# Row-tiling the w_phi folds of a one-core attention and feed-forward kernel

## The chip, the cores and the metric

One Trainium2 chip, one core. The metric is the device time of one execution in microseconds (us). All executions quoted here were in the same (fast) state, at a granted TensorE clock of 0.999 to 1.0 of full speed. The kernel before takes 288.41 us in the median of six runs (287.72 to 289.37).

PE is TensorE (matmuls), PEld its weight loads, DVE VectorE, ACT ScalarE, SP SyncE, which only issues DMAs here.

## The reference, cut to what matters

```python
# A: linear attention with a learned feature map, 32 heads of 20 features; B: gated feed-forward
pq = einsum("bhsd,hdf->bhsf", q, w_phi)      # the same for k
phi_q = concat([softmax(pq), softmax(-pq)])
...
out = g * A(x) + (1 - g) * B(x)              # x is 2048 x 640
```

The kernel never computes q. It folds w_phi into the projection weights once: wq2 = wq @ BD, where BD holds the 20 x 20 block of each head on its diagonal. This fold is small: five row blocks of 128 rows for k and five for q. After it come the projections, the attention state, the feed-forward products (gate, up, down), and the attention output, which joins the down product.

## The kernel before: the parts that the change and the argument touch

One fold multiplies a 128-row block of weights by BD. The 640 features are five groups of 128, and 128 is no multiple of 20, so a group touches seven or eight heads. Heads 0 to 15 go to one bank of the result memory (PSUM), heads 16 to 31 to another; the middle group is split. The function, simplified:

```python
def fold(self, kt, which, banks, ekey):
    for i in range(self.KD):                       # 5 feature groups of 128
        lo, hi = self.HLO[i], self.HHI[i]          # heads that the group touches
        for h in (0, 1):                           # two banks
            a, z = max(lo, 16 * h), min(hi, 16 * h + 15)
            if a > z: continue
            n = (z - a + 1) * DH                   # 140 columns, 80 for the split group
            matmul(bank(banks[h])[:, c0:c0 + n], wT[:, i, kt*P:(kt+1)*P], self.BD[:, i, k0:k0 + n], ...)
    # then one copy out of PSUM (an evacuation), by VectorE ("d") or ScalarE ("a")
```

The order around the folds (v_early and k_early are projections, 128-row matmuls):

```python
self.v_early(4, 6); self.v_early(5, 0)
f(0, "k", (2, 3), "d"); f(1, "k", (4, 5), "a")
self.v_early(6, 6)
f(2, "k", (2, 3), "d"); f(3, "k", (4, 5), "a"); f(4, "k", (0, 1), "d")
self.v_early(7, 6); self.k_early(0, 2)
f(0, "q", (4, 5), "d"); f(1, "q", (6, 7), "d")
self.k_early(1, 0)
f(2, "q", (4, 5), "d"); f(3, "q", (6, 7), "d")
self.k_early(2, 2)
f(4, "q", (4, 5), "d")
...                                              # k_early(3), then pq: the q projections
```

For each of 16 row tiles, `num(t)` computes the attention numerator on PE (64-row matmuls), normalises it on DVE, about 4 us, and issues a DMA that transposes the result into goT. The output matmuls of the tile read goT later. The list `at` says at which of the 148 steps of a stage of four tiles (185 in the last) a numerator is put; a step is two matmuls and takes 0.135 us.

```python
def num(self, t):
    ...                                          # 20 matmuls, 11 VectorE operations
    sc.dma("sp", lambda e: e.dma_start_transpose(self.goT[:, gs, :, :], self.Og[:, sl, :]), ...)

def first_nums(idx):                             # in the second gate and up stage
    if idx in (4, 8):
        self.num(idx // 4 - 1)                   # tiles 0 and 1
...
at = (1, 31, 61, 91)
for b in range(self.NB):
    downs(b, {at[k]: 4 * b + 2 + k for k in range(4 if b < 3 else 2)})
```

The softmax here doesn't subtract the row's maximum and nothing guards it: scores larger than these inputs give would overflow.

## Time and profile before

| quantity | value | where it stands |
|---|---|---|
| time | 288.41 us | median of 6 runs |
| PE busy | 281.2 of 286.9 us | the table of busy time |
| folds, first to last | 13.8 to 24.3 us | the line of the folds, L332 |
| down stage, first to last matmul start | 197.93 to 283.88 us: 85.95 us | single records |

Four lines from the page of the kernel before: the span, busy time with its share and the number of instructions, then the chain of work that ended last, as shares of the span by engine and by line (L352 are the projections and the gate and up products, L714 the down and output products, L658 the numerators, L332 the folds).

```profile
span 286.9 us, 7006 instructions
PE 281.2 (98%) x3017; PEld 185.5 (65%) x3032; DVE 174.7 (61%) x353; ACT 105.0 (37%) x199; POOL 5.3 (2%) x36
...
PE 93%; SPq 3%; DMA 2%; ACT 1%; issue 1%; ACTq 0%
PE ps L352 60%; PE ps L714 28%; PE ps L658 2%; DMA xT<-in_A_x_dram 2%; PE ps L450 2%; SPq L221 2%; PE ps L332 1%; SPq L234 1%; SPq L225 1%; ACT Ek L414 0%; ACT Eq L519 0%; SPq L217 0%; ACT outsb L727 0%; ACT gcol L417 0%; ACTq L42 0%
```

The kernel is bound by PE, and the folds hold 1% of the chain. Next, PE's timeline around the folds: start, duration, form, count; a bracket shows idle time and what ended it.

```profile
13.84 0.79 PE L332 MATMUL ps<-BD,wkT 128*128 128x140 bf16 x12
14.80 1.53 PE L352 MATMUL ps<-w,xT 128*128 128x512 bf16 x10 [0.18 <-DMA xT<-in_A_x_dram]
16.18 1.11 PE L332 MATMUL ps<-BD,wkT 128*128 128x140 bf16 x18
...
20.01 0.80 PE L332 MATMUL ps<-BD,wqT 128*128 128x140 bf16 x12
20.65 1.53 PE L352 MATMUL ps<-w,xT 128*128 128x384 bf16 x10
22.01 0.79 PE L332 MATMUL ps<-BD,wqT 128*128 128x140 bf16 x12
22.64 1.52 PE L352 MATMUL ps<-w,xT 128*128 128x384 bf16 x10
```

The pair of folds at 20.01 us occupies PE for 0.64 us, the one at 22.01 us for 0.63 us. The last view is PE's timeline at a place that the prediction never looked at, the first use of the fourth row tile's goT in the down stage:

```profile
211.07 0.57 PE L714 MATMUL ps<-wo_sb,goT 64*128 64x320 bf16 x6
211.47 0.56 PE L658 MATMUL ps<-KV,Eq 64*128 64x88 bf16 x20
```

There is no bracket: PE waits for nothing. But the transpose that fills this goT was issued at 207.92 us and landed at 210.52 us, and its first reader starts at about 211.1 us. The margin is 0.55 us, and here the loss will begin. Single records of the same trace show two things more. One tile has less margin: the sixteenth, 0.16 us (landed at 275.15 us, first read at 275.32 us). And six of the sixteen transposes already took 3.2 to 4.2 us to land, all at tiles with enough margin.

### The profile page before, as it was taken

How to read it: one execution, taken by the hardware profiler on the slowest of the kernel's cores; microseconds unless marked ns; L12 is line 12 of the kernel's file. 1: busy time of each engine (PE TensorE's matmuls, PEld its weight loads, DVE VectorE, ACT ScalarE, POOL GpSimd, SP SyncE). 2: the span in 40 equal slices, each digit the busy share in tenths (PEclk: the TensorE clock that was granted, in tenths of full speed). 3: DMA queues.
4: the chain of work that ended last, by engine and by line, in shares of the span. 5: the costliest groups of instructions: out<-in, count | busy, mean ns of one | idle time of the engine just before them, and what ended most of it. 6: DMA issues, size and time to landing. Idle time of an engine off the chain costs nothing.

```text
span 286.9 us, 7006 instructions
## 1 busy us (share of the span) xinstructions
PE 281.2 (98%) x3017; PEld 185.5 (65%) x3032; DVE 174.7 (61%) x353; ACT 105.0 (37%) x199; POOL 5.3 (2%) x36
## 2 busy tenths in 40 slices
PE   8999999999999999999999999999999999999996
PEld 3666689999994444444444444445777777777785
DVE  3248999999977553567242334225883883883801
ACT  3367887677663322322323223221112112112111
POOL 7000000000000000000000000000000000000000
PEclk9999999999999999999999999999999999999999
DMA  8999995000002000011000000000232333422221
GB/s 226 206 187 247 367 367 174 0 2 2 2 0 48 0 0 0 3 24 23 2 0 0 0 2 0 0 2 0 25 94 62 35 48 92 49 49 85 56 72 48
DMA packets 36937, 18.67 MB, mean 65 GB/s; under 512 B 28970, under 2 KB 36394, under 8 KB 36906
## 3 DMA queue, kind: packets, MB, share of 16 engines
q1 hardware_dynamic: 36096, 17.86, 26.1%
q8 instruction: 24, 0.39, 0.6%
q10 hardware_dynamic: 810, 0.35, 0.5%
q14 instruction: 7, 0.06, 0.1%
HBM read 9.04 MB, written 2.62 MB: 41 GB/s over the span
## 4 chain that ended last, share of the span: by engine, by line
PE 93%; SPq 3%; DMA 2%; ACT 1%; issue 1%; ACTq 0%
PE ps L352 60%; PE ps L714 28%; PE ps L658 2%; DMA xT<-in_A_x_dram 2%; PE ps L450 2%; SPq L221 2%; PE ps L332 1%; SPq L234 1%; SPq L225 1%; ACT Ek L414 0%; ACT Eq L519 0%; SPq L217 0%; ACT outsb L727 0%; ACT gcol L417 0%; ACTq L42 0%
## 5 line engine op out<-in xcount | busy, mean ns | idle before, releaser
L352 PE MATMUL ps<-xT,wg_sb 128*128 128x512 bf16 (+1 forms) x265 | 63.8, 379 | 0.4 <-issue 0.2
L352 PE MATMUL ps<-xT,wu_sb 128*128 128x512 bf16 (+1 forms) x263 | 63.3, 379 | 0.5 <-DVE hT L632 0.2
L630 ACT ACTIVATE gl<-ps 128x512 bf16<-128x512 f32 x52 | 30.9, 596 | 73.1 <-PE ps L352 68.7
L632 DVE TENSOR_TENSOR hT<-ps,gl 128x512 bf16<-128x512 f32 x39 | 26.7, 690 | 38.6 <-PE ps L352 38.5
L714 PE MATMUL ps<-wd_sb,hT 64*128 64x320 bf16 x648 | 49.5, 296 | 0.0
L352 PEld LDWEIGHTS ps<-xT,wu_sb 128*128 128x128 bf16 (+1 forms) x270 | 26.5, 99 | 29.8 <-DVE hT L632 0.5
L352 PEld LDWEIGHTS ps<-xT,wg_sb 128*128 128x128 bf16 (+1 forms) x270 | 26.2, 99 | 29.0 <-ACT gl L630 0.2
L352 PE MATMUL ps<-w,xT 128*64 128x512 bf16 (+6 forms) x398 | 41.6, 325 | 0.4 <-DMA xT<-in_A_x_dram 0.2
L727 ACT ACTIVATE outsb<-ps,Gm 128x320 bf16<-128x320 f32 (+2 forms) x31 | 14.5, 515 | 72.4 <-PE ps L714 72.4
L352 PEld LDWEIGHTS ps<-w,xT 128*64 128x64 bf16 (+1 forms) x400 | 35.8, 107 | 5.1 <-DMA xT<-in_A_x_dram 0.4
L714 PEld LDWEIGHTS ps<-wd_sb,hT 64*128 64x128 bf16 x648 | 31.0, 94 | 12.1 <-issue 0.4
L714 PE MATMUL ps<-wo_sb,goT 64*128 64x320 bf16 (+2 forms) x340 | 27.8, 288 | 0.0
L352 PE MATMUL ps<-xT,wq 128*64 128x512 bf16 (+1 forms) x184 | 26.1, 381 | 0.4 <-ACT Eq L519 0.3
L434 DVE TENSOR_TENSOR Ek<-Ek,Dk 128x640 bf16<-128x640 bf16 x32 | 25.0, 822 | 0.6
L685 DVE TENSOR_TENSOR O<-ps,RH 128x640 bf16<-128x640 f32 x32 | 24.8, 816 | 0.0
L425 DVE TENSOR_REDUCE Dk<-Ek 128x64 f32<-128x1280 bf16 x16 | 23.7, 1479 | 0.1
L519 ACT ACTIVATE Eq<-ps 128x512 bf16<-128x512 f32 x40 | 21.7, 605 | 1.1 <-PE ps L352 0.8
L414 ACT ACTIVATE Ek<-ps 128x640 bf16<-128x640 f32 x32 | 20.7, 703 | 3.6 <-PE ps L352 3.6
L632 DVE TENSOR_TENSOR xT<-ps,gl 128x512 bf16<-128x512 f32 x13 | 9.0, 691 | 18.2 <-PE ps L352 18.2
L714 PEld LDWEIGHTS ps<-wo_sb,goT 64*128 64x128 bf16 x340 | 16.1, 94 | 5.4
L352 PEld LDWEIGHTS ps<-xT,wq 128*64 128x64 bf16 (+1 forms) x185 | 15.3, 109 | 3.4 <-ACT Eq L519 0.8
L714 PE MATMUL ps<-wd_sb,xT 64*128 64x320 bf16 (+2 forms) x270 | 16.7, 269 | 0.0
(69 smaller groups left out, 173.2 us busy)
## 6 DMA issues: line engine op xcount, KB each, us to landing
out_dram<-outsb SPq DMA_DIRECT2D x7, 320.0 KB, 2.3
wd_sb<-in_B_w_down_dram SPq DMA_DIRECT2D x1, 2080.0 KB, 14.3
wg_sb<-in_B_w_gate_dram SPq DMA_DIRECT2D x1, 1120.0 KB, 5.7
wu_sb<-in_B_w_up_dram SPq DMA_DIRECT2D x1, 1120.0 KB, 8.2
wg_sb<-in_B_w_gate_dram SPq DMA_DIRECT2D x1, 960.0 KB, 9.8
wu_sb<-in_B_w_up_dram SPq DMA_DIRECT2D x1, 960.0 KB, 10.4
w<-in_A_wqkv_dram SPq DMA_DIRECT2D x5, 160.0 KB, 4.7
wo_sb<-in_A_wo_dram SPq DMA_DIRECT2D x1, 800.0 KB, 9.7
```

What stands on the lines that cost most here:

```text
L221: sc.dma("sp", lambda e: e.dma_start_transpose(T[:, :, :], self.wqkv[:, c0:c0 + D]), writes=[key])
L352: self.sc.op("pe", lambda e: e.matmul(self.ps[a:z, bank * 512 + c0:bank * 512 + c0 + n], lhs[:, a:z], rhs, start=first, stop=fin), reads=r ...
L414: self.sc.op("act", lambda e, s=s, scale=scale: e.activation(self.Ek[:, se, s, :], self.ps[:, o:o + self.D], AF.Exp, scale=scale), reads=[ ...
L425: sc.op("dve", lambda e: e.tensor_reduce(self.Dk[:, se, 0, :].rearrange("p (s h) -> p s h", h=H), self.Ek[:, se, :, :].rearrange("p s (h d ...
L434: sc.op("dve", lambda e, v=v, r=r: e.tensor_tensor(v, v, r, ALU.mult), reads=[("Rk", se)], writes=[("Ek", se, s)])
L450: sc.op("pe", lambda e: e.matmul(self.ps[a:a + 64, b * 512 + c:b * 512 + c + 2 * nf], va[:, lo:lo + 64], self.Ek[:, se, :, f0:f0 + nf], st ...
L519: sc.op("act", lambda e, s=s, scale=scale: e.activation(self.Eq[:, s, i, b * self.BT:(b + 1) * self.BT], self.bank(bank), AF.Exp, scale=sc ...
L630: sc.op("act", lambda e: e.activation(self.gl[:, slot, :], self.bank(banks[0]), AF.Gelu_apprx_tanh), reads=[("ps", banks[0])], writes=[("g ...
L632: sc.op("dve", lambda e: e.tensor_tensor(hT, self.bank(banks[1]), self.gl[:, slot, :], ALU.mult), reads=[("ps", banks[1]), ("gl", slot)], ...
L685: dve(lambda e, o=o, f=f, s=s: e.tensor_tensor(o, V[s][:, :, :, 0:DH], f, ALU.mult), rb + [key(6 + s)], [("O", s, sl)], guard=old)
L714: sc.op("pe", lambda e: e.matmul(self.bank(bk, w), lhs, rhs, start=opens and x == 0, stop=end and not opens, skip_group_check=True), reads ...
L727: sc.op("act", lambda e: e.activation(dst, self.bank(bk, w), AF.Copy, scale=g), reads=rd, writes=wr)
```

## The change

Its intent: cut the 640 features into ten units of 64. A unit lies within four heads, so a matmul has 64 rows and exactly 80 columns, and two of them, on the two halves of the array, can run side by side. The change never lets the halves write one bank at once: in the first three pairs the upper half writes the bank of heads 0 to 15 and the lower half the other, and in the last two pairs they change banks; before that, PE waits on its own semaphore for the end of the first three. Going over from 128-row to 64-row matmuls, or back, is what the prediction calls a mode switch. To have other work during that wait, two or three row blocks form a group. The last q fold keeps the old form.

```diff
+    def folds(self, kts, which, banks, ekeys):
+        for first, units in ((True, ((0, 5), (2, 7), (4, 9))), (False, ((6, 1), (8, 3)))):
+            for kt, bk in zip(kts, banks):
+                for x, us in enumerate(units):
+                    for r, u in enumerate(us):
+                        i, lo = u // 2, 16 * u // 5
+                        b, c0, k0, fin = bk[u // 5], (lo % 16) * DH, (lo - self.HLO[i]) * DH, x == len(units) - 1
+                        q = 64 * r
+                        sc.op("pe", lambda e: e.matmul(
+                            self.bank(b)[:, c0:c0 + 4 * DH], wT[q:q + 64, i, kt * P:(kt + 1) * P],
+                            self.BD[q:q + 64, i, k0:k0 + 4 * DH], start=first and x == 0, ...),
+                            ..., after=[("turn", b)] if x == 0 and not first else ())
+        for kt, bk, ek in zip(kts, banks, ekeys):
+            self.fold_evac(kt, which, bk, ek)
...
-        f(0, "k", (2, 3), "d")
-        f(1, "k", (4, 5), "a")
+        self.folds((0, 1), "k", ((2, 3), (4, 5)), "da")
         self.v_early(6, 6)
-        f(2, "k", (2, 3), "d")
-        f(3, "k", (4, 5), "a")
-        f(4, "k", (0, 1), "d")
+        self.folds((2, 3, 4), "k", ((2, 3), (4, 5), (0, 1)), "dad")
...
-        f(0, "q", (4, 5), "d")
-        f(1, "q", (6, 7), "d")
+        self.folds((0, 1), "q", ((4, 5), (6, 7)), "dd")
         self.k_early(1, 0)
-        f(2, "q", (4, 5), "d")
-        f(3, "q", (6, 7), "d")
+        self.folds((2, 3), "q", ((4, 5), (6, 7)), "dd")
```

More of the change, by code (lines that the diff above doesn't have):

```diff
@@ L317, in gate_column @@
               reads=[("ps", b)], writes=["wgate"])
+    def folds(self, kts, which, banks, ekeys):
+        sc = self.sc
+        DH = self.DH
+        wT = self.wkT if which == "k" else self.wqT
+        for first, units in ((True, ((0, 5), (2, 7), (4, 9))), (False, ((6, 1), (8, 3)))):
[7 more added lines that the diff above has]
+                            self.bank(b)[:, c0:c0 + 4 * DH], wT[q:q + 64, i, kt * P:(kt + 1) * P],
+                            self.BD[q:q + 64, i, k0:k0 + 4 * DH], start=first and x == 0, stop=fin and not first,
+                            skip_group_check=True),
+                            reads=["w%sT" % which, ("BD", i)], signal=fin,
+                            writes=[("ps", b)] + ([("turn", b)] if fin else []),
+                            after=[("turn", b)] if x == 0 and not first else ())
+        for kt, bk, ek in zip(kts, banks, ekeys):
+            self.fold_evac(kt, which, bk, ek)
     def fold(self, kt, which, banks, ekey):
@@ L335, in fold, with fold_evac @@
                     reads=["w%sT" % which, ("BD", i)], writes=[("ps", b)], signal=fin)
+        self.fold_evac(kt, which, banks, ekey)
+    def fold_evac(self, kt, which, banks, ekey):
         src = self.pair(banks)
```

## The prediction

> **What bounds the kernel now.** One core, 288.56 us (median of 3). The busy table shows PE 281.2 us of a 286.9 us span (98%), and the chain that ended last is 93% PE. The folds of w_phi (line L332) are only 60 of 3017 matmuls, between 13.8 and 24.5 us. In the chain they hold 0.94 + 0.73 + 0.63 + 0.32 us, and another 0.63 us before it: about 3.2 us, 1.1% of the span.
>
> **Costs, from single records of the trace.** A 128-row fold starts 60 ns after its predecessor for 140 columns and 35 ns for 80: six matmuls (4 x 140, 2 x 80) take 315 ns per row block. The kernel already holds the new shape: the numerator's 64-row matmuls of 88 columns (L658) start as pairs, 3 ns apart, one pair each 39 ns. For 80 columns I estimate 36 ns, so five pairs are 180 ns per block: 135 ns less. Nine blocks change (the last q fold stays), 1.2 us of PE time at most.
>
> **What is added.**
> 1. Mode switches. The Trainium skill, "TensorEngine Tiling (Array Packing)", Key Properties, says that changing the tiling mode drains the engine. The trace agrees: where one numerator stands alone among 128-row matmuls (118.5 to 119.4 us), the first pair starts 311 ns after the last 512-column matmul instead of 216 (+95), and the next 128-row matmul 134 ns after the last pair instead of 39 (+95), plus some 20 ns of slower first starts: about 0.21 us per group, four groups.
> 2. Changing banks. The second half of a block waits for PE's own semaphore from the end of the first half: about 195 ns of matmul plus some 55 ns of release, by estimate 325 ns after the block's first pair. A group of two has only 216 ns of other work: about 110 ns, then 30 ns of stall. A group of three covers nearly all (about 70 ns).
> Sum: a group of two costs about 0.72 us against 0.63 (+0.09); the group of three about 0.82 against 0.945 (-0.12).
>
> **What is critical.** k(0,1) ends before a wait for the x transpose (PE idle until 14.80 us): absorbed. k(2,3,4) is followed by a projection that needs ScalarE's copy of v (ends 17.13 us; weights load at 17.18): its gain is lost. q(0,1) starts at 20.0 us on the DMA of wqT, which hides its entering drain: about even. q(2,3): evacuations of q(0,1) now start some 0.08 us later so VectorE frees banks 6, 7 at about 22.24 us, where the group wants them at 22.2: a further 0.1 us of stall; the group ends about 0.17 us late. After that ScalarE waits for PE (0.32 us at 25.9) and PE is full to the end, so the delay passes through.
>
> **Predicted:** 288.7 us (+0.15), range 288.1 to 289.4; faster by over 2% 0.005, within 2% 0.99, slower by over 2% 0.005.
>
> **What would show it.** Pairs 36 ns apart; about 95 ns lost on entering and leaving each group; stalls of about 0.1 us in the middle of groups of two, on PE's own semaphore; PE still starting near 14.80, 17.18 and 20.0 us; pq's first matmul at about 26.05 instead of 25.9 us.
>
> **What would make it wrong.** A self-wait much longer than 250 ns (each 0.1 us adds 0.2 on the critical q groups); a gain after 20 us; a time spread between runs (288.14 to 289.37) larger than the effect.

## More of the kernel before

The view of the transposes' line, L690, gives their spread:

```profile
DMA to landing us min/median/max: 2.6/2.6/4.2
```

## The result, and the profile after

290.32 us in the median (289.96 to 290.74, six runs), against 288.41 us of before. The ratio is 1.0067, 95% interval 1.0047 to 1.0086. Ratios here and below are the mean time of one kernel's fast runs over that of the other's of the same rounds, so not quite the ratio of the medians quoted. It is a slowdown of about 1.9 us: "within 2%" holds, but the time lies outside the range.

The span and busy line of the page after:

```profile
span 289.1 us, 7069 instructions
PE 282.5 (98%) x3053; PEld 196.0 (68%) x3068; DVE 174.9 (60%) x353; ACT 105.1 (36%) x199; POOL 5.3 (2%) x36
```

PE is busy 1.3 us longer. First the place that was changed, PE's timeline (L378 are the projections now):

```profile
14.65 0.73 PE L332 MATMUL ps<-BD,wkT 64*128 64x80 bf16 x20
15.31 1.53 PE L378 MATMUL ps<-w,xT 128*128 128x512 bf16 x10
16.77 0.84 PE L332 MATMUL ps<-BD,wkT 64*128 64x80 bf16 x30
...
20.52 0.73 PE L332 MATMUL ps<-BD,wqT 64*128 64x80 bf16 x20
21.17 1.54 PE L378 MATMUL ps<-w,xT 128*128 128x384 bf16 x10
22.64 0.79 PE L332 MATMUL ps<-BD,wqT 64*128 64x80 bf16 x20
23.37 0.82 PE L378 MATMUL ps<-w,xT 128*128 128x384 bf16 x4
```

All starts are some 0.5 to 0.8 us later than before, but this is already so at 14.65 us, before any change took effect. It stems from the first microseconds: the 20 transposes of x start 56 ns apart in the profile before, and 107 ns apart until 5.7 us in the profile after. Over thirteen profiles, the last of these transposes starts anywhere from 5.36 to 6.60 us, in padded and unpadded kernels alike. The Trainium skill, "TensorE: Matmul & The Clock Gate", Part 1, describes it: a free-running window decides when the clock goes from half to full, so the moment varies between runs; the 107 and 56 ns spacings of this trace are those it gives. It is noise, so absolute times must not be compared across profiles. Distances inside a profile can be: from the first q fold to the first pq matmul, 5.89 us before (20.01 to 25.90) and 6.12 us after (20.52 to 26.63).

Then the place where the time went. The list of PE's waits, the whole kernel: first before, then after. The columns are the total in us, how often, and the longest.

```profile
PE ps L541 <- DVE zero L537: 1.2, 1, 1.2
PE ps L352 <- ACT Eq L519: 0.3, 1, 0.3
PE ps L352 <- DVE hT L632: 0.2, 1, 0.2
PE ps L352 <- DMA xT<-in_A_x_dram: 0.2, 1, 0.2
PE ps L352 <- issue: 0.2, 1, 0.2
```

```profile
PE ps L735 <- DMA goT<-Og: 1.8, 2, 1.3
PE ps L567 <- DVE zero L563: 1.2, 1, 1.2
PE ps L378 <- ACT Eq L545: 0.3, 1, 0.3
PE ps L378 <- ACT vaug L432: 0.3, 1, 0.3
PE ps L378 <- issue: 0.2, 1, 0.2
```

Two lines are new. One, 0.3 us for vaug, ScalarE's copy of v, stands beside the folds, where the prediction had seen it coming. The other is the surprise: PE now waits for goT, some 188 us after the last fold. In PE's timeline after, at the place shown of before:

```profile
211.64 0.30 PE L735 MATMUL ps<-wo_sb,goT 64*128 64x320 bf16 x1
213.28 0.58 PE L735 MATMUL ps<-wo_sb,goT 64*128 64x320 bf16 x5 [1.33 <-DMA goT<-Og]
```

The fourth tile's transpose was issued at 208.15 us: 0.23 us later than before by the clock of the profile, where PE's work stands 0.58 us later, so if anything it was early. But it landed after 5.08 us, not 2.60 us. The same view as of before, for L711:

```profile
DMA to landing us min/median/max: 2.6/2.6/5.1
```

What was different? The view of the DMA queues from 207 to 213 us, before and then after. The digits are busy tenths of the DMA engines in slices of 0.15 us; a queue's line has packets, MB and share; the last line has the count of transposes and the median time to landing in us:

```profile
DMA  0000000010000069999400000000003000000000
...
q1 hardware_dynamic: 672, 0.16, 13.7%
q8 instruction: 1, 0.02, 1.0%
q14 instruction: 1, 0.01, 0.3%
...
goT<-Og SPq DMA_TRANSPOSE x2, 2.6
```

```profile
DMA  0000000000000062999990000000027000000000
...
q1 hardware_dynamic: 672, 0.16, 42.7%
q14 instruction: 1, 0.01, 1.8%
q8 instruction: 1, 0.02, 1.5%
...
goT<-Og SPq DMA_TRANSPOSE x2, 3.8
```

Two queues of kind "instruction" carry blocks of the engines' own programs. On q8 they are 16,384 bytes, one for about every 256 instructions of PE; on q14 8,192 bytes, and those of the stretch in question come about 129 instructions of VectorE apart. Before, VectorE's block (208.31 us) and PE's (211.62 us) pass on either side of the transpose's packets, which run from about 209 to 210 us. After, both fall into them: PE's at 209.24 us for 1.48 us, VectorE's at 210.00 us for 1.76 us. The same 672 packets on q1 then took 42.7% of the engines' time, not 13.7%.

The change moved the blocks: it adds 36 matmuls with their weight loads to PE's program, 72 instructions, and takes 7 waits (semaphore instructions, 127 to 120) from VectorE's, as one wait now covers both banks of a fold, and 2 from ScalarE's: 63 more in all, as the page says (7006 to 7069). So from the folds on, every block border falls on other work. The Trainium skill, "Runtime: NRT & Kernel Launch", Instruction fetch mechanics, has the programs refilled in 16 KiB blocks of 256 instructions by a DMA queue, and calls the cost of a border "mostly hidden". For PE the trace has the same block; the question is whether hidden holds.

### The profile page after: what moved, and what is told of

The parts are those of the page before. It is cut to its first block, busy times and chain, and to the rows that moved or that the text cites. A ratio compares the mean times of both kernels' runs of the same rounds, so it can differ in the third digit from the quotient of the medians.

```text
span 289.1 us, 7069 instructions
## 1 busy us (share of the span) xinstructions
PE 282.5 (98%) x3053; PEld 196.0 (68%) x3068; DVE 174.9 (60%) x353; ACT 105.1 (36%) x199; POOL 5.3 (2%) x36
## 5 line engine op out<-in xcount | busy, mean ns | idle before, releaser
L378 PE MATMUL ps<-xT,wg_sb 128*128 128x512 bf16 (+1 forms) x265 | 63.8, 379 | 0.4 <-issue 0.2
L378 PE MATMUL ps<-xT,wu_sb 128*128 128x512 bf16 (+1 forms) x263 | 63.3, 379 | 0.4
L735 PE MATMUL ps<-wd_sb,hT 64*128 64x320 bf16 x648 | 51.8, 296 | 0.0
L378 PEld LDWEIGHTS ps<-xT,wu_sb 128*128 128x128 bf16 (+1 forms) x270 | 26.6, 99 | 29.5
L378 PEld LDWEIGHTS ps<-xT,wg_sb 128*128 128x128 bf16 (+1 forms) x270 | 26.2, 99 | 29.0 <-ACT gl L651 0.2
L735 PEld LDWEIGHTS ps<-wd_sb,hT 64*128 64x128 bf16 x648 | 37.1, 94 | 7.7 <-issue 0.4
L378 PE MATMUL ps<-w,xT 128*64 128x512 bf16 (+6 forms) x398 | 41.7, 325 | 0.4 <-ACT vaug L432 0.3
L378 PEld LDWEIGHTS ps<-w,xT 128*64 128x64 bf16 (+1 forms) x400 | 35.7, 107 | 5.1 <-ACT vaug L432 0.2
L735 PE MATMUL ps<-wo_sb,goT 64*128 64x320 bf16 (+2 forms) x340 | 31.0, 288 | 1.8 <-DMA goT<-Og 1.8
L378 PE MATMUL ps<-xT,wq 128*64 128x512 bf16 (+1 forms) x184 | 26.2, 380 | 0.4 <-ACT Eq L545 0.3
L735 PEld LDWEIGHTS ps<-wo_sb,goT 64*128 64x128 bf16 x340 | 20.6, 94 | 4.9 <-DMA goT<-Og 2.4
L378 PEld LDWEIGHTS ps<-xT,wq 128*64 128x64 bf16 (+1 forms) x185 | 15.3, 108 | 3.4 <-ACT Eq L545 0.8
L735 PE MATMUL ps<-wd_sb,xT 64*128 64x320 bf16 (+2 forms) x270 | 17.4, 269 | 0.0
```

The costliest lines, as they stand in the source:

```text
L378: self.sc.op("pe", lambda e: e.matmul(self.ps[a:z, bank * 512 + c0:bank * 512 + c0 + n], lhs[:, a:z], rhs, start=first, stop=fin), reads=r ...
L735: sc.op("pe", lambda e: e.matmul(self.bank(bk, w), lhs, rhs, start=opens and x == 0, stop=end and not opens, skip_group_check=True), reads ...
```

## Experiments

Theory (fetch): nothing in the folds costs 1.9 us; program blocks that now collide with tight transposes do. Rival (folds): the row-tiled folds, or the shift of work after them, cost it. In the kernels below, empty semaphore increments, on a semaphore that nobody waits for, fill the programs so that the block borders move and the work does not. All results were correct. All padding is put into the third gate and up stage, unless said otherwise:

```diff
-        gateups(2, none)
+        pads = [self.nc.alloc_semaphore("pad_pe"), self.nc.alloc_semaphore("pad_dve")]
+        def pad(idx):                                    # called after each of 14 chunks
+            for eng, sem, n in ((self.nc.tensor, pads[0], 72), (self.nc.vector, pads[1], 121)):
+                for _ in range(n * (idx + 1) // 14 - n * idx // 14):
+                    eng.sem_inc(sem, 1)
+        gateups(2, pad)
```

The down stage is given as the distance from its first to its last matmul's start, in the profile. The medians of before in the four sets of rounds were 288.41 (with after), again 288.41 (b_pe72_dve121, b_pe256_dve128, a_pe184_dve7, a_early), 288.02 (b_pe72, b_dve121, a_dve7, b_pe256_thin) and 288.46 us (a_early2, b_early, b_early_pad); the ratios take them into account.

| kernel | median us | ratio to before, 95% | waits for goT | down stage us |
|---|---|---|---|---|
| before | 288.41 | | none | 85.95 |
| after | 290.32 | 1.0067 (1.0047 to 1.0086) | 1.8 | 88.28 |
| b_pe72_dve121 | 289.88 | 1.0055 (1.0031 to 1.0080) | 1.8 | 88.25 |
| b_pe72 | 289.47 | 1.0046 (1.0029 to 1.0063) | 1.2 | 87.97 |
| b_dve121 | 287.95 | 0.9999 (0.9984 to 1.0014) | none | 86.00 |
| b_pe256_dve128 | 297.35 | 1.0311 (1.0289 to 1.0333) | none | 85.95 |
| b_pe256_thin | 288.23 | 1.0007 (0.9992 to 1.0022) | none | 85.95 |
| a_pe184_dve7 | 288.27 | 0.9997 (0.9977 to 1.0017) | none | 85.95 |
| a_dve7 | 288.71 | 1.0027 (1.0008 to 1.0047) | 0.4 | 86.87 |
| a_early | 288.08 | 0.9986 (0.9959 to 1.0014) | none | 85.56 |
| a_early2 (the same) | 288.69 | 1.0009 (0.9995 to 1.0023) | none | 85.56 |
| b_early | 288.56 | 1.0013 (0.9997 to 1.0030) | none | 85.56 |
| b_early_pad | 288.06 | 0.9987 (0.9970 to 1.0003) | none | 85.55 |

### b_pe72_dve121: old folds, new block borders

The kernel before with the edit shown above.

> The kernel before, folds untouched, with 72 empty semaphore increments on PE and 121 on VectorE, spread over the gate and up products of the third row stage. 72 is what the change added to PE's program (36 matmuls with their weight loads), 121 is 128 minus the 7 waits it took from VectorE's, so from there on the blocks in which the two programs are fetched (16 KB on PE, 8 KB on VectorE) start at the same work as in the kernel after. Fetch theory (the loss is a fetch of program blocks that falls on the transposes of goT): PE waits for goT for 1 to 2 us, as after (1.8 us), and the time is 289.6 to 290.4, against 288.4 of before. Rival (the folds themselves, or the shift of work that they cause, cost the 1.9 us): 288.4 +- 0.5, no wait for goT.

Measured: 289.88 us, ratio 1.0055. Its first waits:

```profile
PE ps L714 <- DMA goT<-Og: 1.8, 2, 1.2
```

The same two waits at the same two tiles, the transpose of the fourth tile landing after 4.97 us (after: 5.08), a down stage as long as after's within 0.03 us. The folds of this kernel are those of before. The rival falls.

### b_pe256_dve128: a control that failed

`n` is 256 on PE and 128 on VectorE.

> Control: the kernel before with one whole block of empty increments on each engine (256 on PE, 128 on VectorE) at the same place, so the block borders fall on the same work as before. If the increments cost nothing by themselves, both theories say 288.4 +- 0.5 and no wait for goT. If it is slower, the increments cost time and the other padded runs must be read against this one.

Measured: 297.35 us. The profile shows why, in PE's waits:

```profile
PE ps L352 <- issue: 5.8, 12, 0.8
PE ps L352 <- ACT gl L638: 1.6, 1, 1.6
```

All but two of these gaps (0.4 us in both) stand in the padded stretch, in front of gate products: 18 or 19 increments in a row on PE, with 9 or 10 on VectorE, are too many to hide there. No run tried which of the two it is, but the trace says it. From 150 us PE's increments follow each other every 151 ns without a pause: 18 or 19 take 2.7 to 2.9 us, and the ten matmuls of a chunk only 2.16 us. VectorE's start 93 ns apart, and VectorE idles over 2 us before each of its operations there. Outside the stretch the kernel does what was expected, 85.95 us of down stage and no wait for goT. As a control of the time it is worthless.

### b_pe256_thin: the control mended

The same padding over two stages, 9 or 10 increments on PE and 4 or 5 on VectorE at each place:

```diff
-        gateups(2, none)
-        gateups(3, none)
+        gateups(2, pad)      # 28 places, 256 and 128 increments in all
+        gateups(3, pad)
```

> The control mended: one whole block on each engine as before, but spread over two gate and up stages (9 increments on PE and 4 or 5 on VectorE at each place, not 18 and 9), as thin as in the run with 72 and 121, where the padded stretch took no longer. If so: no gap on PE in the padded stretch, no wait for goT, 288.4 +- 0.5.

Measured: 288.23 us, 1.0007, no gap in the padded stretch. Increments as thin as this cost nothing, and whole blocks change nothing.

### a_pe184_dve7: new folds, old block borders

The kernel after, `n` is 184 (72 + 184 = 256) and 7.

> The kernel after with 184 empty increments on PE (72 + 184 = 256) and 7 on VectorE: folds row-tiled, but block borders in the down stage where the kernel before has them. Fetch theory: the waits for goT (1.33 and 0.45 us) are gone or under 0.3 us in total, time 288.4 to 289.0. Rival (folds): 290.3 +- 0.4 with the padding, as after.

Measured: 288.27 us, 0.9997, no wait for goT. PE's timeline at the critical place:

```profile
211.63 0.57 PE L735 MATMUL ps<-wo_sb,goT 64*128 64x320 bf16 x6
212.03 0.56 PE L679 MATMUL ps<-KV,Eq 64*128 64x88 bf16 x20
```

More instructions in the program, and 2 us less time. With the borders put back, the row-tiled kernel is as fast as before.

### Which of the two fetches: b_pe72, b_dve121, a_dve7

`n` is (72, 0), (0, 121), and (0, 7) in the kernel after.

> The kernel before with the 72 increments on PE alone; VectorE's block borders stay where they were. If PE's 16 KB fetch is the main cause: the transposes of the fourth and eighth row blocks land some 1.5 us later than 2.6 us after issue, PE waits 0.7 to 1.1 us and about 0.5 us for them, time 289.4 to 289.9. If both fetches must meet: the first wait is under 0.5 us, time under 289.2.

> The kernel before with the 121 increments on VectorE alone; PE's block borders stay. If PE's fetch is the main cause: the 8 KB fetch alone delays one transpose by 0.5 us or less, PE waits for goT at most 0.4 us, time 288.2 to 288.8. If VectorE's fetch is the main cause: a wait of about 1 us, 289.4 to 289.9.

> The kernel after with 7 increments on VectorE alone, so that its block borders are those of before while PE's stay those of after. If PE's fetch is the main cause: waits for goT of 0.7 to 1.1 us and 0.45 us remain, time 289.6 to 290.1 (after: 290.3). If VectorE's fetch is: the first wait is gone, 288.9 or less.

PE's borders alone cost most of it: b_pe72 loses 1.45 us (289.47 against 288.02 us in those rounds). But not at the tiles that I had expected: the fourth tile's transpose lands after 3.41 us and is hardly waited for (its first reader starts 0.3 us later than in b_pe256_thin), the eighth (4.52 us) and the twelfth (4.15 us) are, 0.80 and 0.42 us. VectorE's borders alone cost nothing: one transpose lands after 3.50 us and its margin takes all but 0.06 us of it. In the kernel after, putting back VectorE's 7 instructions removed the 1.33 us wait, leaving 0.42 us, and 288.71 us: better than the 289.6 to 290.1 that I had expected. (Its four runs spread from 288.28 to 289.56 us, and the profile is of the fastest.) The waits of b_pe72 and of a_dve7:

```profile
PE ps L714 <- DMA goT<-Og: 1.2, 2, 0.8
PE ps L735 <- DMA goT<-Og: 0.4, 1, 0.4
```

So the two costs do not add. The two landings of about 5 us are cases in which both fetches fell on one transpose; PE's fetch alone reached 4.52 us.

### a_early, b_early, b_early_pad: transposes off the edge

One numerator more goes into the second gate and up stage, so each transpose is issued some 30 steps (4 us) sooner.

```diff
-            if idx in (4, 8):
+            if idx in (4, 8, 12):
...
-            downs(b, {at[k]: 4 * b + 2 + k for k in range(4 if b < 3 else 2)})
+            downs(b, {at[k]: 4 * b + 3 + k for k in range(4 if b < 3 else 1)})
```

> The kernel after with each numerator one place earlier (three instead of two in the second gate and up stage), so that every goT is issued about 30 steps, 4 us, sooner. Fetch theory: a transpose that lands 2.5 us late is no longer waited for; no wait for goT; one more change of tiling mode costs 0.2 us: 288.5 to 289.1. Rival (folds, or slower row-tiled matmuls in the down stage): 290.3 or a little more.

> The kernel before with each numerator one place earlier, as in a_early. Before waits for no goT, so nothing is to be gained; one more change of tiling mode costs 0.2 us: 288.0 to 288.7, ratio to before 0.999 to 1.003. Down stage as long as in a_early (85.6 us).

> a_early again, beside b_early: both are deaf to late transposes, so their difference is the folds alone. The profiles of before and after say 0.23 us more between the first q fold and the first pq, 0.17 us less at one wait of the gate and up stage: 0 to +0.3 us against b_early, within the noise. If the folds cost more than 0.5 us here, something else is hidden.

> The kernel before with numerators one place earlier and the padding (72, 121) that cost 1.5 us in b_pe72_dve121. If what the padding costs is the wait for late transposes: no wait for goT and the time of b_early +- 0.4. If the shifted fetches also hurt elsewhere: over 0.6 us slower than b_early.

The kernel after with this edit: 288.08 us, and 288.69 us when run again, no wait for goT. The fetches still meet transposes (landings up to 3.8 us), but nobody waits. The edit gains nothing on the kernel before (b_early, 1.0013), and it makes the harmful padding harmless: b_early_pad 288.06 us against 289.88 us without it. a_early2 beside b_early, 1.0009 against 1.0013, is the folds alone: no difference within about 0.2%.

No version beats before beyond the noise, so none is recommended for speed.

### Every transpose of every profile

The thirteen profiles hold 208 transposes of goT. 84 had no program fetch running in the 2.5 us after their issue: they landed in 2.56 to 2.65 us, all of them. 124 had one; 77 of these took over 2.9 us, up to 5.08 us. By queue: with a block on q14 alone 9 of 22 were that late (up to 3.6 us), with PE's alone 59 of 93 (up to 4.52 us), with both all 9 (2.92 to 5.08 us). An obvious rival, the kernel's own writes of its output, falls: 33 of the 84 had such a write under way in those 2.5 us, and none was late. This is a count over what was recorded, not an intervention, but together with the padded kernels, in which only the borders moved, it leaves little else.

## Why the prediction was wrong, point by point

- The costs of the folds were right. Pairs start 36 ns apart (predicted 36). Entering a group costs 95 to 97 ns over the usual spacing (predicted 95), leaving it about 103 (predicted 95). In a group of two, the second half of the first block starts 179 ns after the last pair instead of 36, and the next block waits 29 ns more: 172 ns of stall (predicted 140). In the group of three, 35 + 30 + 29 ns (predicted about 70).
- The groups: by single records, q(0,1) takes 0.66 us from its start to the next matmul (predicted about even with 0.64), q(2,3) 0.82 us with its entry, against 0.63 us (predicted +0.17, measured +0.19). From the first q fold to pq this is +0.23 us.
- What DMA and ScalarE absorb was partly right. Where the front ran late, as in the profile after, x had landed and the first wait was gone: from the first k fold to pq it is then 11.99 us, against 11.61 us of old folds in a profile without that wait, +0.38 us. A wait for hT of 0.2 us at 125 us, in before, is absent after (from the first gate product to the first down matmul 119.13 and 118.96 us). The sum of the two is +0.2 us; b_early and a_early2 show the same, 269.78 and 270.01 us from the first fold to the last matmul. That this is near the predicted +0.15 us is partly luck: the k groups cost 0.15 us that were thought to be absorbed, and the wait for hT, which the prediction did not mention, gave 0.17 us back.
- The step that failed: "After that ScalarE waits for PE (0.32 us at 25.9) and PE is full to the end, so the delay passes through", and the list under "What is added", which has two costs, mode switches and changing banks. The delay did pass through. But the change also moved the block borders of two programs, and so the fetches, against work that had not changed. In the down stage that is 88.28 us instead of 85.95 us: +2.3 us in the profile, where +0 was predicted. The two waits are 1.8 us of it; after each PE stands a further 0.16 us behind, and the last 0.2 us are three small steps back (two of 0.08 us, one of 0.06 us at the end) that no run explains. I had read "PE is full" as "nothing else is near": the margins of the transposes, 0.55 us at the fourth tile and 0.16 us at the sixteenth, can be read from the trace before, and the fetch packets stand in the DMA table of its page. I looked at neither.
- The list of what could make the prediction wrong (a longer self-wait, a cheaper switch, noise) did not contain the cause.

Shown: the loss follows the block borders and not the folds (two kernels with the borders exchanged, one clean control, b_pe256_thin, and one of use for the down stage alone, b_pe256_dve128), and it runs through late transposes (moving them earlier removes it). Argued only: that the packets wait for one another on shared DMA engines. The Trainium skill, "Trainium Kernel Development and Optimization", Key Constraints, says of the queues of SP, ACT and POOL that they all run on the same 16 engines and interleave; it does not speak of the fetch queues, and the trace here does not name the engine of a packet. Also open: why VectorE's small fetch matters so much only together with PE's.

## What to carry to other kernels

When a change adds or takes instructions, the borders at which each engine's program is fetched move for all later work, and a transfer that was just in time can become late: look up the margin of every recurring transfer, from landing to first use, and the spread of its landings, before trusting that the rest of the trace only shifts. Here the tightest margin, 0.16 us at the sixteenth tile, was never hit: its transpose landed after 2.56 to 2.57 us in every run with this order of numerators, so the loss depended on where the blocks happened to fall. When an effect appears far from the edit, pad the programs by a whole block less what the change added, thinly, and see whether it goes away. A verdict of half a per cent on one version is not a verdict on the idea: here the same folds gave 1.0067 and 0.9997.

## What the Trainium skill lacked or had wrong

- "Runtime: NRT & Kernel Launch", Instruction fetch mechanics: it calls the cost of a block border mostly hidden. Here, moved borders alone cost 1.5 us of 288 (b_pe72_dve121, 1.0055), through DMA transposes that landed after up to 4.97 us instead of 2.6 us. Nothing on the page warns of this.
- The same section: blocks of 16 KiB (256 instructions). PE's fetches are 16,384 bytes, as it says; those on the queue that serves VectorE are 8,192 bytes, about 129 of its instructions apart.
- "TensorEngine Tiling (Array Packing)", Key Properties, says that changing the tiling mode drains the engine, with no cost. Here it was 95 to 103 ns each way between matmuls that otherwise follow at once.
- The same page, Instruction Overhead: about 60 cycles of overhead for each matmul. It does not show in the spacing of starts: 80-column matmuls of 128 rows start 35 ns apart, and row-tiled ones in pairs 36 ns apart, the two of a pair 3 to 9 ns.
- No page that I read has the price of a semaphore increment among matmuls: 13 or 14 in a row on PE after each chunk of ten 512-column matmuls cost nothing (a_pe184_dve7); 18 or 19 lengthened the gate and up stages by 9.3 us over 14 places (b_pe256_dve128). In a row they start 151 ns apart.
